# Landing margins in a planner's model, and an earlier place for the attention: a windowed-attention and MLP kernel on one Trainium2 core

## The chip, the cores and the metric

The kernel runs on one core of one Trainium2 chip. The core has five engines, each with its own instruction stream that is worked off in order: TensorE (PE) for matrix products and transposes, VectorE (DVE), ScalarE (ACT), GpSimd (POOL) and SyncE (SP). SP here only issues transfers (DMA); POOL issues transfers too. An instruction that waits for a semaphore holds everything behind it on the same engine. Inputs lie in HBM, work is done in the on-chip SBUF, and products arrive in eight PSUM banks of 2 KiB per partition.

The metric is the device time of one launch in microseconds (us). The median of three runs before the change is 238.64 us (238.53 to 239.28).

## The reference

The inputs are `q`, `k`, `v` of shape (4, 8, 768, 64): 4 batches, 8 heads, 768 positions, head size 64. Then come two weights, `moe_w_in` (512 x 2048) and `moe_w_out` (2048 x 512).

```
scores = q @ k^T / sqrt(64)
keep   = (key < 4) or (0 <= query - key < 128)      # 4 sink keys and a window of 128
a      = softmax(where(keep, scores, -1e9))
x      = (a @ v), heads side by side: 3072 tokens x 512
out    = relu(x @ w_in)^2 @ w_out                   # 3072 x 512, float32
```

## The kernel before, in words

**Work.** A batch is worked in three parts `s` = 0, 1, 2 of 256 positions. For a part and a half of the heads (`m0` = 0 or 2: two pairs of heads `m`), the kernel forms the scores of the window only (`scores`, L571, PE), takes the exponential of each pair (L590, ACT), multiplies it by the triangle mask (`domask`, L599 on DVE or L221 on POOL), forms the values together with a column of ones that gives the denominator (`values`, L632, PE), and divides (`norm`, L643 and L644, DVE). The four sink keys of all heads are gathered into a small block `kblk` (`sink_keys`, L509, two small DVE copies), scored against all later queries by one product (`sink_scores`, L530, PE), and their exponentials `es` (L539, ACT) join `values` for `s` > 0. The result `xn_sb` has to be transposed into `xT`. Then `layer1` (L691, PE; relu L700; square L707) makes the hidden values for parts 0 and 1 together (512 tokens, eight steps) and for part 2 (256 tokens, four steps), and `layer2` (L731) makes the output in 24 steps of four matmuls each per batch, which are copied out and stored (L747).

**Two ways to get q, k and v in.** Batches 0 and 1 load them as float32 through SP (L339, L355), cast them, and transpose on PE (L468); their `xn_sb` is transposed on PE too (`bridge`, L668). Batches 2 and 3 (`NATURAL`) take another way: POOL loads them with a cast in the transfer (`load_natural`, L372 for q and k into `qn`, L381 for v; 18 transfers a batch), SP transposes each of 12 tiles by a transfer (`turn`, L426, `qkT<-qn`), and SP transposes `xn_sb` by a transfer as well (`turn_x`, L655, `xT<-xn_sb`, two per part; in the planner the second one comes after the first has landed).

**What sets the order.** Nothing is scheduled by hand or by the compiler. The kernel describes its steps as `Op`s in a `Plan`, each with the engines that can do it and their costs in us, the steps it comes after, the PSUM and SBUF slots that it takes and gives back, and a key. `Plan.run` simulates time: again and again it picks, among the steps whose predecessors are done, the one that can start earliest, and among equal starts (to 0.01 us) the one with the lowest key. The step is then emitted, so the order of picking is the order of every engine's stream on the chip. A step's end in the model decides when its readers can be picked. For a transfer the model takes the issue, then `DMA_START` (1.2 us on SP, 1.6 on POOL), then its own duration on its queue (0.3 us for a transpose, 64 x 0.032 = 2.05 us for a natural load), and then `DMA_LATENCY` = 0.9 us. A transpose is thus seen as landed 1.25 + 1.2 + 0.3 + 0.9 = 3.65 us after its issue begins.

**Keys.** Batch `b` has `layer1` at `b` to `b` + 0.5 and `layer2` at `b` + 0.5 to `b` + 1, 1/48 of a batch per step. The attention of batch `b` + 1 is woven into this, with a place `f` of each step between 0 and 1.05 and the key `b` + LO + (HI - LO) x `f`, LO = 0.05 and HI = 0.9. For part `s` and half `m0`, `scores` have `f` = 0.36 + `s`/6 + 0.08 `m0`, `values` 0.16 more, and `turn_x` of the part stands at 0.36 + `s`/6 + 0.36. `sink_keys` stand at 0.1, `sink_scores` at 0.4. The attention of batch 1 has keys of its own, without LO and HI.

Of the kernel before, what the change touches and what calls it, by code (L numbers as in the profile page):

```python
# [19 lines left out]
DMA_LATENCY = 0.9  # L20
# [3 lines left out]
class Slot:  # L24
# [3 lines left out]
    def __init__(self, pools, readers):  # L28
        self.pools = (pools,) if isinstance(pools, str) else pools
        self.pool, self.readers, self.end = self.pools[0], readers, 0.0  # L30


class Op:
    def __init__(self, key, engines, run, after, takes, reads, dma, follow):
        self.key, self.engines, self.run = key, engines, run
        self.after, self.takes, self.reads, self.dma = list(after), list(takes), list(reads), dma
        self.follow, self.yields = list(follow), []
        self.end = self.issued = None


class Plan:

# [12 lines left out]
    def run(self):  # L57
        free = {p: [0.0] * n for p, n in self.capacity.items()}
        engine = {}
        queue = {}  # L60
        waiting = list(self.ops)
        blockers = {id(o): len(o.after) + len(o.follow) for o in waiting}
        landed = {}
        users = {}
        for o in waiting:
            for a in o.after + o.follow:
                users.setdefault(id(a), []).append(o)
        ready = [o for o in waiting if not blockers[id(o)]]
        for o in ready:
            o.at = 0.0  # L70
        left = len(waiting)
        while left:
            best = None
            for o in ready:
                t = o.at
                need = {}
                for s in o.takes:
                    if len(s.pools) > 1:
                        s.pool = min(s.pools, key=lambda p: min(free[p], default=1e9))
                    need[s.pool] = need.get(s.pool, 0) + 1  # L80
                ok = True
                for p, n in need.items():
                    if len(free[p]) < n:
                        ok = False
                        break
                    t = max(t, sorted(free[p])[n - 1] + LATENCY)
                if not ok:
                    continue
                if o.dma:
                    past = landed.get(next(iter(o.engines)), ())  # L90
                    if len(past) >= 8:
                        t = max(t, past[-8])
                pick = None
                for e, c in o.engines.items():
                    slack = PE_SLACK if e == "pe" and t > 0 else 0.0
                    start = max(t + slack, engine.get(e, 0.0))
                    if pick is None or start + c < pick[1] + pick[2]:
                        pick = (e, start, c)
                cand = (round(pick[1], 2), o.key)
                if best is None or cand < best[0]:  # L100
                    best = (cand, o, pick)
            assert best is not None, "no op can run"
            _, o, (e, start, cost) = best
            ready.remove(o)
            left -= 1
            for s in o.takes:
                free[s.pool].sort()
                free[s.pool].pop(0)
            self.now, self.gap = start, start - engine.get(e, 0.0)
            o.run(e)  # L110
            engine[e] = start + cost
            end = start + cost
            if o.dma:
                moved = [y.end - DMA_LATENCY for y in o.yields]
                queue[e] = max([queue.get(e, 0.0), end + DMA_START[e]] + moved) + o.dma
                end = queue[e] + DMA_LATENCY
                landed.setdefault(e, []).append(end)
            o.end, o.issued = end, start + cost
            for s in o.reads:
                s.readers -= 1  # L120
                s.end = max(s.end, end)
                if not s.readers:
                    free[s.pool].append(s.end)
            for u in users.get(id(o), ()):
                blockers[id(u)] -= 1
                if not blockers[id(u)]:
                    u.at = max([a.end + LATENCY for a in u.after] + [a.issued for a in u.follow])
                    ready.append(u)
        return max(o.end for o in self.ops)
# [3 lines left out]
def kernel(  # L133
# [145 lines left out]
    def dma_op(queue, name, run, us, behind=None, takes=(), yields=()):  # L279

        def go(e):
            ds = run(e)
            if behind is not None:
                for d in ds:
                    after_dma(d, loaded[behind])
            loaded[name] = ds[-1]
        o = op(-5, {queue: (0.85 if queue == "pool" else 0.5) + (0.3 if behind else 0.0)}, go, dma=us, takes=takes,
               follow=[chained[queue]] if queue in chained else (),
               after=[ops[behind]] if behind is not None else ())
        ops[name] = chained[queue] = o  # L290
        o.yields += [ops[y] for y in yields]
        o.follow += [ops[y] for y in yields]
        return o
# [17 lines left out]
    ops, late = {}, {}  # L311
# [48 lines left out]
    def load_natural(b, s, older_values):  # L360

        begun = [ops["layer1", b - 2, 0, 0], w_out_op[3]]
        for ti in (1, 0):
            if s == 0:
                qn_slot[b, ti] = Slot("qr", NT)
            for i in range(2):
                t = 2 * s + i

                def run(e, t=t, ti=ti):
                    if t == 0:  # L370
                        qn_t[b, ti] = work["qr"].tile([128, NT, DM], BF16, name="qn", tag="qr")
                    return [nc.gpsimd.dma_start(  # L372
                        out=qn_t[b, ti][:, t, :].rearrange("p (h d) -> p h d", d=D),
                        in_=(q, k)[ti][b, :, 128 * t:128 * t + 128, :].rearrange("h p d -> p h d"))]
                o = dma_op("pool", ("qk", b, ti, t), run, 64 * 0.032,
                           ("v", 1, 3) if (b, ti, t) == (2, 1, 0) else None,
                           [qn_slot[b, ti]] if t == 0 else ())
                o.after += begun
        for t in (2 * s, 2 * s + 1):
            def run(e, t=t):  # L380
                return [nc.gpsimd.dma_start(  # L381
                    out=v_sb[b % 2][:, t, :, 0:D],
                    in_=v[b, :, 128 * t:128 * t + 128, :].rearrange("h p d -> p h d"))]
            o = dma_op("pool", ("v", b, t), run, 64 * 0.032)
            o.after += begun + older_values

    def load_sinks(queue, b):
        eng = nc.scalar if queue == "act" else nc.sync
# [3 lines left out]
    def attention(b, key):  # L392
# [16 lines left out]
        def stage(g, f0, f1, side):  # L409
# [9 lines left out]
            if b in NATURAL:  # L419
                for s in range(NS):  # L420
                    for ti in (1, 0):
                        for i in range(2):
                            t = 2 * s + i

                            def turn(e, s=s, ti=ti, i=i, t=t):
                                nc.sync.dma_start_transpose(  # L426
                                    out=qkT_sb[:, :, ti, t, :], in_=qn_t[b, ti][:, t, :])
                            ops["turn", b, ti, t] = op(
                                at(0.1 * s), {"sp": 1.25}, turn, dma=0.3, reads=[qn_slot[b, ti]],
                                after=[ops["qk", b, ti, t]] + prev_scores + prev_sinks)  # L430
                            copies.append(ops["turn", b, ti, t])
                    ops["cast", b, s] = ops["v", b, 2 * s + 1]
            w = 2 if b == 0 else 1
# [112 lines left out]
            for s in range(t0 // 256, last // 256):  # L546
                fs = 0.36 + 0.5 * (256 * s - t0) / (last - t0)
                norms = []
                for m0 in (0, 2):
# [36 lines left out]
                    o = 0 if s else 128  # L586
# [65 lines left out]
                if b in NATURAL:  # L652
                    for t in (2 * s, 2 * s + 1):
                        def turn_x(e, t=t):
                            nc.sync.dma_start_transpose(out=xT[:, t // 2, :, 128 * (t % 2):128 * (t % 2) + 128],  # L655
                                                        in_=xn_sb[:, t, :])
                        o_ = op(at(fs + 0.36), {"sp": 1.25}, turn_x, dma=0.3, after=norms + older_layer1 +
                                ([o_] if t % 2 else []))
                    ops["bridge", b, s] = ops["xT", b, s] = o_
                    continue  # L660
                bx = Slot(side, 1)
# [132 lines left out]
    for b in range(1, B):  # L794
        load_sinks("sp", b)

    LO, HI = 0.05, 0.9
    for b in range(B):
        if b == 0:
            at = attention(0, lambda f: f - 1.0)  # L800
# [62 lines left out]
```

## Time and profile before

| what | value |
|---|---|
| median of three runs | 238.64 us (238.53 to 239.28) |
| the profiled execution: its time, its span | 240.36 us, 238.7 us |
| PE busy | 220.0 us, 92% of the span |
| ACT, DVE, POOL busy | 113.0, 103.8, 57.2 us |
| mean granted TensorE clock | 0.981 |
| longest waits of PE | 4.2 us (on `xn_sb`), 3.0 us (on `xT`) |

The span runs from the first to the last instruction of the profiled execution; its time is 1.66 us longer than the span, and 1.72 us longer than the median of the runs. The time axis of every row that is quoted is the profiled execution's, in us from the start of the span. By that axis batch 0 begins its MLP at about 19 us, batch 1 at 84, batch 2 at 139.5 and batch 3 at 188.

In rows that name a wait, the part behind `<-` is what ended it. `DMA a<-b` is a transfer that writes tile a from b, counted from its issue to its landing. `SPq` is SP's issuing of transfers.

### The profile page before, as it was taken

How to read it: one execution, taken by the hardware profiler on the slowest of the kernel's cores; microseconds unless marked ns; L12 is line 12 of the kernel's file. 1: busy time of each engine (PE TensorE's matmuls, PEld its weight loads, DVE VectorE, ACT ScalarE, POOL GpSimd, SP SyncE). 2: the span in 40 equal slices, each digit the busy share in tenths (PEclk: the TensorE clock that was granted, in tenths of full speed). 3: DMA queues.
4: the chain of work that ended last, by engine and by line, in shares of the span. 5: the costliest groups of instructions: out<-in, count | busy, mean ns of one | idle time of the engine just before them, and what ended most of it. 6: DMA issues, size and time to landing. Idle time of an engine off the chain costs nothing.

```text
span 238.7 us, 4545 instructions
## 1 busy us (share of the span) xinstructions
PE 220.0 (92%) x1918; PEld 140.0 (59%) x1940; DVE 103.8 (44%) x186; ACT 113.0 (47%) x126; POOL 57.2 (24%) x85
## 2 busy tenths in 40 slices
PE   7889999999983999999999869999999999999991
PEld 6458984568851655596455444578545545784440
DVE  6563435359755357455316414466403323340010
ACT  2495565427882085575334444759403346550110
POOL 5184016033986507982002000000000000000000
PEclk9999999999998899999999979999999999999998
DMA  5999969999999999999844732010005312000051
GB/s 170 270 180 208 214 169 202 276 368 215 228 146 118 152 158 193 165 151 132 56 88 127 149 122 44 3 29 18 0 0 136 109 23 91 0 0 3 0 220 45
DMA packets 84101, 29.70 MB, mean 124 GB/s; under 512 B 70256, under 2 KB 80496, under 8 KB 84080
## 3 DMA queue, kind: packets, MB, share of 16 engines
q0 software_dynamic: 40128, 8.92, 43.4%
q1 hardware_dynamic: 43912, 20.48, 38.2%
q8 instruction: 15, 0.25, 0.5%
q14 instruction: 6, 0.05, 0.1%
q10 hardware_dynamic: 40, 0.01, 0.0%
HBM read 27.30 MB, written 6.29 MB: 141 GB/s over the span
## 4 chain that ended last, share of the span: by engine, by line
PE 65%; DMA 19%; ACT 5%; SPq 4%; DVE 3%; issue 2%; ACTq 0%; DVEq 0%; POOLq 0%
PE pm L691 29%; PE py L731 25%; PE po L632 5%; DMA qr<-in_q_dram 5%; DMA qr<-in_k_dram 4%; DMA qkT<-qn 4%; PE ps L571 3%; DMA w_out_sb<-in_moe_w_out_dram 2%; DMA qn<-in_k_dram 2%; ACT r L700 2%; DMA vf<-in_v_dram 2%; ACT expm L590 2%; SPq L339 2%; SPq L426 1%; DMA xT<-xn_sb 1%
## 5 line engine op out<-in xcount | busy, mean ns | idle before, releaser
L691 PE MATMUL pm<-xT,w_in_sb 128*128 128x256 bf16 (+1 forms) x576 | 88.2, 311 | 3.2 <-DMA xT<-xn_sb 3.0
L731 PE MATMUL py<-w_out_sb,gT 128*128 128x512 bf16 x365 | 87.0, 382 | 1.8 <-issue 0.8
L691 PEld LDWEIGHTS <-w_in_sb 128*128 128x128 bf16 x576 | 63.0, 114 | 24.2 <-issue 5.4
L700 ACT ACTIVATE r<-pm 128x1024 bf16<-128x1024 f32 x48 | 49.2, 1026 | 43.6 <-PE pm L691 35.2
L731 PEld LDWEIGHTS <-gT 128*128 128x128 bf16 x384 | 35.8, 98 | 40.0 <-issue 2.7
L590 ACT ACTIVATE expm<-ps 128x1024 bf16<-128x1024 f32 (+1 forms) x48 | 43.3, 955 | 18.1 <-PE ps L571 18.1
L707 DVE TENSOR_TENSOR gT<-r 128x1024 bf16<-128x1024 bf16 x48 | 33.4, 696 | 42.3 <-ACT r L700 42.3
L599 DVE TENSOR_TENSOR expm<-expm,mask 128x1024 bf16<-128x1024 bf16 (+1 forms) x37 | 24.2, 662 | 22.4 <-ACT expm L590 21.8
L205 ACT ACTIVATE osb<-py 128x1024 f32<-128x1024 f32 (+1 forms) x10 | 9.6, 960 | 39.6 <-PE py L731 33.0
L632 PEld LDWEIGHTS <-expm 128*128 128x128 bf16 x352 | 18.0, 101 | 5.5 <-issue 1.6
L632 PE MATMUL po<-v,expm 128*128 128x65 bf16 x352 | 19.1, 198 | 0.3 <-DVE v L207 0.2
L644 DVE TENSOR_TENSOR xn_sb<-po,rc 128x512 bf16<-128x512 f32 x24 | 16.6, 692 | 0.8
L643 DVE RECIPROCAL rc<-po 128x8 f32<-128x8 f32 x24 | 4.9, 204 | 26.4 <-PE po L632 26.3
L571 PE MATMUL ps<-qkT 64*128 64x128 bf16 (+1 forms) x256 | 14.7, 238 | 0.1
L632 PE MATMUL po<-vs,es 128*128 128x65 bf16 x128 | 14.4, 200 | 0.0
L571 PEld LDWEIGHTS <-qkT 64*128 64x128 bf16 x256 | 8.0, 94 | 10.2 <-issue 9.2
L209 POOL CAST qs<-qr 128x512 bf16<-128x512 f32 (+1 forms) x9 | 6.7, 743 | 29.6 <-DMA qr<-in_k_dram 21.9
L207 DVE COPY osb<-py 128x1024 f32<-128x1024 f32 (+2 forms) x4 | 3.6, 891 | 23.1 <-PE py L731 23.1
L632 PEld LDWEIGHTS <-es 128*128 128x128 bf16 x128 | 12.4, 102 | 0.0
L372 POOL DMA_DIRECT2D qn<-in_k_dram x12 | 10.9, 924 | 2.8 <-DMA vf<-in_v_dram 1.4
L372 POOL DMA_DIRECT2D qn<-in_q_dram x12 | 10.9, 916 | 1.8 <-DMA qn<-in_k_dram 1.8
L381 POOL DMA_DIRECT2D v<-in_v_dram x12 | 10.6, 894 | 2.7 <-DMA qn<-in_q_dram 2.7
(49 smaller groups left out, 99.7 us busy)
## 6 DMA issues: line engine op xcount, KB each, us to landing
out_dram<-osb SPq DMA_DIRECT2D x11, 512.0 KB, 4.6
vf<-in_v_dram SPq DMA_DIRECT2D x12, 256.0 KB, 4.9
w_in_sb<-in_moe_w_in_dram POOLq DMA_DIRECT2D x4, 512.0 KB, 8.1
w_out_sb<-in_moe_w_out_dram POOLq DMA_DIRECT2D x4, 512.0 KB, 10.3
qr<-in_k_dram SPq DMA_DIRECT2D x6, 256.0 KB, 4.3
qr<-in_q_dram SPq DMA_DIRECT2D x6, 256.0 KB, 4.5
qr<-in_k_dram SPq DMA_DIRECT2D x2, 768.0 KB, 5.2
qr<-in_q_dram SPq DMA_DIRECT2D x2, 768.0 KB, 6.8
```

What stands on the lines that cost most here:

```text
L205: nc.scalar.activation(out=dst, in_=src, func=AF.Copy)
L372: return [nc.gpsimd.dma_start(out=qn_t[b, ti][:, t, :].rearrange("p (h d) -> p h d", d=D), in_=(q, k)[ti][b, :, 128 * t:128 * t + 128, :]. ...
L381: return [nc.gpsimd.dma_start(out=v_sb[b % 2][:, t, :, 0:D], in_=v[b, :, 128 * t:128 * t + 128, :].rearrange("h p d -> p h d"))]
L571: nc.tensor.matmul(ps[:, h2, o:o + w], lhsT=qkT_sb[r, m, 1, c, :], rhs=qkT_sb[r, m, 0, qb:qb + w // 128, :], start=(i == 0 and not biased) ...
L590: nc.scalar.activation(out=x[:, :, o:512], in_=bank_t["s", b, s, m][:, :, o:512], func=AF.Exp, scale=scale)
L599: nc.vector.tensor_mul(x[:, :, o:512], x[:, :, o:512], mk[:, :, o:512])
L632: nc.tensor.matmul(pv[:, i, h2, :], lhsT=lhsT, rhs=rhs, start=(n_ == 0), stop=(n_ == len(mms) - 1))
L644: nc.vector.tensor_tensor(out=xn_sb[:, 2 * s:2 * s + 2, 128 * m0:128 * m0 + 256].rearrange("p i (j h d) -> p j i h d", j=2, d=D), in0=pv[: ...
L691: nc.tensor.matmul(pm[:, i, :], lhsT=w_in_sb[:, fb // 4, kb, fb % 4:512:4], rhs=xT[:, c0 // 256:(c0 + cw) // 256, kb, :], start=(kb == 0), ...
L700: nc.scalar.activation(out=r, in_=bank_t.pop(tag), func=AF.Relu)
L707: (nc.vector if e == "dve" else nc.gpsimd).tensor_mul(gT_sb[c0 // 512][:, fbs[0]:fbs[0] + n, c0 % 512:c0 % 512 + cw], r, r)
L731: nc.tensor.matmul(pm[:, i, :], lhsT=gT_sb[t // 4][:, fb, 128 * (t % 4):128 * (t % 4) + 128], rhs=w_out_sb[:, fb, :], start=(fb == 0), sto ...
```

## The change

The planner's `Op` gets a field `margin`, in us, zero unless set, which `Plan.run` adds to the end of a transfer. It is set to 2.0 for every natural load (L372, L381), to 4.0 for every `turn` (L426) and to 1.5 for every `turn_x` (L655). HI goes from 0.9 to 0.75, so the keys of the attention of batches 2 and 3 go over 0.70 of a batch and no longer over 0.85. No instruction is added or removed by this; only the order of the streams, and the choice between two engines where a step has one, can differ.

```
-        self.follow, self.yields = list(follow), []
+        self.follow, self.yields, self.margin = list(follow), [], 0.0
...
                 queue[e] = max([queue.get(e, 0.0), end + DMA_START[e]] + moved) + o.dma
-                end = queue[e] + DMA_LATENCY
+                end = queue[e] + DMA_LATENCY + o.margin
                 landed.setdefault(e, []).append(end)
...
                 o.after += begun
+                o.margin = 2.0
...
             o.after += begun + older_values
+            o.margin = 2.0
...
                             ops["turn", b, ti, t] = op(
                                 at(0.1 * s), {"sp": 1.25}, turn, dma=0.3, reads=[qn_slot[b, ti]],
                                 after=[ops["qk", b, ti, t]] + prev_scores + prev_sinks)
+                            ops["turn", b, ti, t].margin = 4.0
...
                         o_ = op(at(fs + 0.36), {"sp": 1.25}, turn_x, dma=0.3, after=norms + older_layer1 +
                                 ([o_] if t % 2 else []))
+                        o_.margin = 1.5
...
-    LO, HI = 0.05, 0.9
+    LO, HI = 0.05, 0.75
```

More of the change, by code (lines that the diff above doesn't have):

```diff
@@ L36, in __init__ @@
         self.after, self.takes, self.reads, self.dma = list(after), list(takes), list(reads), dma
-        self.follow, self.yields = list(follow), []
+        self.follow, self.yields, self.margin = list(follow), [], 0.0
         self.end = self.issued = None
@@ L115, in run @@
                 queue[e] = max([queue.get(e, 0.0), end + DMA_START[e]] + moved) + o.dma
-                end = queue[e] + DMA_LATENCY
+                end = queue[e] + DMA_LATENCY + o.margin
                 landed.setdefault(e, []).append(end)
@@ L378, in load_natural @@
                 o.after += begun
+                o.margin = 2.0
         for t in (2 * s, 2 * s + 1):
@@ L385, in load_natural @@
             o.after += begun + older_values
+            o.margin = 2.0
     def load_sinks(queue, b):
@@ L430, in stage @@
                                 after=[ops["qk", b, ti, t]] + prev_scores + prev_sinks)
+                            ops["turn", b, ti, t].margin = 4.0
                             copies.append(ops["turn", b, ti, t])
@@ L658, in stage @@
                                 ([o_] if t % 2 else []))
+                        o_.margin = 1.5
                     ops["bridge", b, s] = ops["xT", b, s] = o_
@@ L795 @@
         load_sinks("sp", b)
-    LO, HI = 0.05, 0.9
+    LO, HI = 0.05, 0.75
     for b in range(B):
```

## The prediction, made before the changed kernel was run

> **What bounds the kernel now.** I read the page first, then who waited for whom on PE, then a table of the span by stretches, and last the chain that ended last around the two long waits.
>
> ```profile
> PE 220.0 (92%) x1918; PEld 140.0 (59%) x1940; DVE 103.8 (44%) x186; ACT 113.0 (47%) x126; POOL 57.2 (24%) x85
> ```
>
> ```profile
> PE px L668 <- DVE xn_sb L644: 4.2, 1, 4.2
> PE pm L691 <- DMA xT<-xn_sb: 3.0, 1, 3.0
> ```
>
> PE works 92% of the span; beside its own weight loads, which overlap, nothing reaches half of it, so PE's idle time and slow clock are what an order can win. Two waits stand out, one occurrence each. The table (busy time of PE, PEld, DVE, ACT and POOL, then the granted clock) shows what else is left:
>
> ```profile
> 71.30:75.40 4.10, 0.00 (x0) 0.00 (x0) 1.87 (x6) 0.75 (x1) 3.01 (x4) 1.00 2.44 149
> 75.40:79.20 3.80, 3.68 (x36) 2.53 (x38) 1.23 (x3) 1.02 (x1) 1.80 (x3) 0.56 1.42 103
> 79.20:136.50 57.30, 56.65 (x517) 33.91 (x523) 28.23 (x49) 29.13 (x32) 21.02 (x25) 1.00 1.49 137
> 136.50:139.50 3.00, 0.05 (x2) 0.09 (x1) 1.38 (x3) 2.13 (x3) 0.00 (x0) 1.00 0.47 102
> 139.50:147.20 7.70, 7.69 (x49) 4.32 (x49) 2.12 (x4) 2.05 (x2) 0.00 (x0) 0.78 0.31 92
> ...
> 184.00:196.00 12.00, 11.47 (x80) 5.98 (x79) 3.67 (x6) 5.62 (x6) 0.00 (x0) 1.00 0.28 73
> ```
>
> After each long wait the clock is low (0.56 for 3.8 us, 0.78 for 7.7 us). The quiet stretches idle 0.65 us in 57.3 and 0.53 us in 12.0, so the prize is these two places. PE's own rows there give the waits to two places:
>
> ```profile
> 75.43 0.65 PE L668 MATMUL px<-ident,xn_sb 128*128 128x128 bf16 x8 [4.17 <-DVE xn_sb L644]
> ...
> 139.51 2.40 PE L691 MATMUL pm<-xT,w_in_sb 128*128 128x512 bf16 x8 [2.96 <-DMA xT<-xn_sb]
> ```
>
> The chain at the first:
>
> ```profile
> 64.99 8.44 DMA qkT<-qn
> 73.46 0.16 DVE kblk L509
> ...
> 73.83 0.69 DVE expm L599
> ...
> 74.68 0.70 DVE xn_sb L644
> ...
> 76.08 1.71 PE py L731 x4
> 77.78 1.32 PE po L632 x24
> ...
> 80.13 0.73 PE po L632 x24
> 80.86 1.73 PE py L731 x8
> ```
>
> Batch 2's first transpose lands 8.44 us after its issue. `sink_keys` of batch 2 stands on DVE ahead of a mask and a norm of batch 1, and waits for that landing. The mask, the norm and then PE's transposes of batch 1 stand behind it, though none needs it. On DVE and ACT:
>
> ```profile
> 73.46 0.35 DVE L509 COPY kblk<-qkT 64x16 bf16<-64x16 bf16 x2 [4.60 <-DMA qkT<-qn]
> ```
>
> ```profile
> 67.33 1.95 ACT L590 ACTIVATE expm<-ps 128x1024 bf16<-128x1024 f32 x2
> 70.11 1.94 ACT L590 ACTIVATE expm<-ps 128x1024 bf16<-128x1024 f32 x2 [0.84 <-PE ps L571]
> ```
>
> DVE was idle from 73.46 - 4.60 = 68.86, and the mask's exponential, the first of the two from 67.33, was done at about 68.3. The second place:
>
> ```profile
> 127.31 0.55 PE ps L571 x12
> ...
> 129.69 0.73 PE po L632 x24
> ...
> 133.08 1.22 SPq L655
> ...
> 134.39 1.22 SPq L426
> ...
> 135.70 1.22 SPq L426
> ...
> 136.97 2.50 DMA xT<-xn_sb
> ...
> 141.92 1.32 PE po L632 x24
> 143.24 3.97 PE pm L691 x16
> ```
>
> `layer1` of batch 2 needs the four `turn_x` of parts 0 and 1. The last `values` of part 1 (129.69) are late; then SP issues one `turn_x` at 133.08, two turns of batch 3, and the last `turn_x` at 136.97, which lands 2.50 us later. PE had nothing else left by then: it is busy for 0.05 us of the stretch from 136.5 to 139.5.
>
> **The change, part by part.** *What is added or removed:* no instruction. All that follows is order.
>
> *Price of the first wait.* PE stood 4.17 us, from 71.26 to 75.43. The four matmuls behind it took 1.71 us where eight take 1.73, so 0.85 too much; the 24 of `values` took 1.32 where the later 24 took 0.73, 0.59 too much. Together 4.17 + 0.85 + 0.59 = 5.61 us.
>
> *Margins on loads and turns.* In the planner's model, `sink_keys` become ready 2.0 (the natural load of k) + 4.0 (the turn) = 6.0 us later. The old model gives a turn 3.65 us; the trace gave 8.44. So the model took the landing for 4.79 us earlier than it was, in the trace's time at 73.43 - 4.79 = 68.6, which is just where DVE began to idle. With 6.0 more it is 74.6, after the true landing. In the 4.60 us from 68.86 DVE then finds the mask (0.69), reciprocal and norm (from the mask's end at 74.52 to 75.38, 0.86) and two masks whose exponentials end at 70.11 + 1.94 = 72.05: two times 0.69 more. These 2.9 us fit before 74.6, so I expect all of them to pass `sink_keys`. What is late next: `sink_keys` run at about 73.5 to 74.6 with nothing of batch 1 behind them that PE already waits for, since the norm then behind them needs `values`, which need those masks. PE finds `xn_sb` ready at 68.86 + 0.69 + 0.86, about 70.4, before it asks at 71.26. From both sides: nothing is gained if `sink_keys` stay in front, 5.61 us if the wait goes. I take 5.61, because the shift (6.0) is larger than the model's error (4.79).
>
> The same 6.0 us move everything else that reads a turn of batches 2 and 3, `scores` and `sink_scores`. Could that starve a later step? The rows:
>
> ```profile
> 104.97 0.86 PE pk L530 x4
> ...
> 119.88 0.73 PE po L632 x24
> ...
> 147.21 0.86 PE pk L530 x4
> ...
> 167.19 0.72 PE po L632 x24
> ```
>
> The sink scores of batch 2 run 14.9 us before the first `values` that use them (119.88, part 1), those of batch 3 20.0 us before (167.19). Six us later still leaves 9 and 14, so I cost it at nothing; without that cover it would be up to 6 us a batch. Where PE comes 5.61 us earlier to the sink scores, being placed later protects it from the last turns of batch 2. On POOL the loads are modelled as landed 2.0 us later, so a mask there may pass one load issue; on SP, stores and `turn_x` may pass a turn. Both only shift work that has us to spare (in the row from 136.5 POOL does nothing any more).
>
> *HI from 0.9 to 0.75, and the margin on `turn_x`.* Price of the second wait: PE stood 2.96 us; then 8 matmuls of the same 512 columns took 2.40 for 1.73, 0.67 too much; 24 of `values` 1.32 for 0.73, 0.59; 16 matmuls 3.97 for twice 1.73, 0.51. With 2.96 that is 4.73 us.
>
> The last `values` of part 1 stand at f = 0.36 + 0.167 + 0.16 + 0.16 = 0.847. Their key falls by 0.15 x 0.847 = 0.127 of a batch, 6.1 steps of `layer2` (1/48 each) of 0.86 us (1.73 for eight matmuls), so 5.3 us earlier against `layer2`; their `scores` move 0.15 x 0.687 x 48 = 4.9 steps. Every instruction of the step moves: six score products a part on PE, exponentials on ACT, masks on DVE or POOL, norms, and the `turn_x` on SP, which come before some turns of batch 3. Against it goes the margin of 1.5: the second `turn_x` of a part is planned after the first has landed, so one more turn (1.22 us) can slip between. Net 5.3 - 1.2 = 4.1 us, against 2.96 needed. Can the engines deliver it? Between the first scores of batch 2 (100.92, next fence) and those of the half in question (123.20) lie three halves, 7.4 us each, while one needs about 0.55 + 1.94 + 0.69 + 0.73 + 0.86 = 4.8 on PE, ACT, DVE, PE and DVE in turn. The room, 3 x 2.6 = 7.8, is more than 5.3. From both sides: nothing, or 4.73. I take 4.73: the same change of batch from 2 to 3 (184 to 196) runs with 0.53 us idle, so a batch change without a wait exists, and I charge that 0.53 here.
>
> ```profile
> 100.92 0.44 PE ps L571 x8
> ...
> 123.20 0.55 PE ps L571 x12
> ```
>
> **Sum.** The profiled execution takes 240.36 us (span 238.7 and 1.66 around it) and the median is 238.64, 1.72 lower. 240.36 - 5.61 - 4.73 + 0.53 = 230.55 profiled; 230.55 - 1.72 = 228.8 for the median.
>
> **The rivals.** *The second wait stays, chance 0.16.* The margins push `scores` of batches 2 and 3 back by as much as HI pulls them forward (6.0 against 5.3 us) and the extra turn on SP does the rest: only the first wait goes, 238.64 - 5.61 = 233.0. For it: the terms are alike in size. Against it: the sink scores wait for all twelve turns of their batch and run at 104.97, so every turn had landed 18 us before the `scores` at 123.20; keys and not landings hold these. The Trainium skill speaks for this rival: "DMA: Bandwidth & Descriptors", section "Anatomy of one DMA — SWDGE (gpsimd) path", gives a transfer a fixed cost of about 2.0 us and its bytes at 436 GB/s, which is an estimate of 2.3 us for a turn's 128 KB, and by it a margin of 4 is time thrown away. The `turn_x` agree with the page, the turns do not, by this table of issues with the median to landing:
>
> ```profile
> qkT<-qn SPq DMA_TRANSPOSE x24, 7.3
> xT<-xn_sb SPq DMA_TRANSPOSE x12, 2.4
> ```
>
> A second rule prices what may remain. The low clock followed a wait of only 2.96 us in these rows, so a remainder of the wait may keep its 1.77 us of slow clock. The Trainium skill, "TensorE: Matmul & The Clock Gate", section "What's actually happening", has the clock fall only after an idle window of about 3.4 us; by it a rest of 2.96 us or less costs itself alone, and this rival would end at 233.0 - 1.77 = 231.2. I give that 0.03 of the 0.16, since the rows speak against it.
>
> *The first wait stays, chance 0.08.* `sink_keys` stay ahead of the mask, because the model of DVE is behind or ahead of the chip at that point: 238.64 - 4.73 + 0.53 = 234.4. For it: only 1.2 us lie between shift and error.
>
> *The change does not do what it says, 0.05.* Other steps fill the same holes and both waits stay: 238.6.
>
> *Slower, 0.09.* The attention is pulled into fewer us than its chain needs, and PE, in order, stands in front of `values` until exponentials and masks are done. From the end of scores at 123.75 the two exponentials and the second mask lead to 126.81, so `values` can't start for 3.06 us:
>
> ```profile
> 124.16 1.94 ACT L590 ACTIVATE expm<-ps 128x1024 bf16<-128x1024 f32 x2
> ```
>
> ```profile
> 126.12 0.69 DVE L599 TENSOR_TENSOR expm<-expm,mask 128x1024 bf16<-128x1024 bf16 x1 [0.23 <-ACT expm L590]
> ```
>
> With only two `layer2` steps (1.73) in between, 1.33 us are left for each of 12 halves in batches 2 and 3: 16.0 us, 244.8. It decides from (5.61 + 4.73 - 0.53) / 12 = 0.82 us a half. Against it: the planner picks by earliest start and puts 1.04 us for an exponential and 0.75 for a mask, above the rows (0.97, 0.69), so it fills this gap before it looks at keys.
>
> **How the numbers follow.** Forecast 0.62, and the four rivals as given. Faster by over 0.3% (0.7 us, about what a measurement of this kernel can tell): 0.62 + 0.16 + 0.08 = 0.86; within it 0.05; slower 0.09. The range begins at 227.0: the sum without the 0.53, and with the 0.65 us of idle in the long quiet stretch gone as well, is 227.6, and durations vary a little. It ends at 235.0 to hold both cases in which one wait stays; that leaves out 0.14.
>
> **What would show it.** In the profile after: the wait of PE for `xn_sb` at 71 gone and no DVE wait of `kblk` on `qkT` over about 1 us; the clock at 1.00 between 72 and 84; `layer1` of batch 1 beginning at about 79; no wait of `layer1` on `xT`, with `layer2` of batch 1 still running when the last `turn_x` of part 1 lands; batch 2's `layer1` beginning near 139.5 - 5.6 - 3.0 = 131. PE's busy time would fall by the slow-clock part, 0.85 + 0.59 + 1.77 = 3.2, to about 217. Wrong would be: a new wait of PE over 1 us on `ps`, `expm` or `qkT` between 85 and 190, or on a turn's landing at `sink_scores`.

## The result, and the profile after

The changed kernel takes 230.12 us (229.33 to 230.80) where the kernel before takes 238.96 us beside it: a ratio of 0.9616, 95% interval 0.9559 to 0.9674. The prediction's 228.8 over 238.64 is 0.9588, inside that interval.

The line of busy times, and who waited on PE, after (the columns as before; the changed file's lines are 3 to 5 higher, so L571 is now L575, L691 is L696, L731 is L736, L426 is L429 and L655 is L659):

```profile
PE 217.9 (95%) x1919; PEld 139.7 (61%) x1940; DVE 104.2 (46%) x186; ACT 113.2 (50%) x126; POOL 57.3 (25%) x85
```

```profile
PE pm L696 <- DMA xT<-xn_sb: 1.0, 1, 1.0
...
PE px L673 <- DVE xn_sb L648: 0.4, 1, 0.4
```

Where waits of 4.2 and 3.0 us stood, 0.4 and 1.0 us are left. The span went from 238.7 to 228.6. The table by stretches (busy time of PE, PEld, DVE, ACT and POOL, then the granted clock):

```profile
71.30:79.00 7.70, 7.08 (x92) 4.47 (x92) 3.19 (x8) 2.99 (x4) 4.67 (x6) 1.00 2.60 120
79.00:131.80 52.80, 52.43 (x484) 31.50 (x486) 27.94 (x47) 29.51 (x33) 21.38 (x26) 1.00 1.66 153
131.80:133.00 1.20, 0.15 (x4) 0.09 (x2) 0.90 (x2) 0.40 (x1) 0.00 (x0) 1.00 0.45 91
133.00:140.00 7.00, 7.00 (x39) 3.57 (x40) 2.50 (x4) 4.37 (x5) 0.00 (x0) 1.00 0.49 131
```

The clock stays at 1.00 behind both places, where it was 0.56 and 0.78. Not all of the profiled gain of 10.1 us belongs to the change. The end is one part: from the last product to the end of the span there were 238.7 - 233.43 = 5.3 us, and now there are 228.6 - 224.26 = 4.3, with nothing in that stretch that the change moves. First the kernel before, then after, in the chain:

```profile
223.76 9.67 PE py L731 x44
```

```profile
214.59 9.67 PE py L736 x44
```

The start of the span adds almost nothing: PE's last four matmuls of `layer2` ahead of the first place start at 70.22 us before and at 70.08 after. PE's rows, before and then after, with the first `layer1` product of batch 1 last:

```profile
70.22 1.04 PE L731 MATMUL py<-w_out_sb,gT 128*128 128x512 bf16 x4
...
84.38 3.62 PE L691 MATMUL pm<-xT,w_in_sb 128*128 128x512 bf16 x16
```

```profile
70.08 1.04 PE L736 MATMUL py<-w_out_sb,gT 128*128 128x512 bf16 x4
...
70.96 0.61 PE L673 MATMUL px<-ident,xn_sb 128*128 128x128 bf16 x8
...
78.86 3.62 PE L696 MATMUL pm<-xT,w_in_sb 128*128 128x512 bf16 x16
```

These rows cut the kernel at three points. Call *stretch 1* the time from the four matmuls to `layer1` of batch 1, and *stretch 2* the time from there to the end of the last product. Stretch 1 fell from 14.16 to 8.78 us, stretch 2 from 149.05 to 145.40. The medians fell by 8.5 (238.64 to 230.12) to 8.8 us.

**The first place.** The chain after:

```profile
65.37 9.39 DMA qkT<-qn
...
74.78 0.16 DVE kblk L513
...
76.24 0.70 DVE xn_sb L648
...
76.99 0.51 PE px L673 x6
...
79.02 3.45 PE pm L696 x16
```

```profile
69.46 0.69 DVE L648 TENSOR_TENSOR xn_sb<-po,rc 128x512 bf16<-128x512 f32 x1
71.03 0.73 DVE L603 TENSOR_TENSOR expm<-expm,mask 128x1024 bf16<-128x1024 bf16 x1 [0.88 <-ACT expm L594]
71.94 0.69 DVE L603 TENSOR_TENSOR expm<-expm,mask 128x1024 bf16<-128x1024 bf16 x1 [0.19 <-ACT expm L594]
74.78 0.35 DVE L513 COPY kblk<-qkT 64x16 bf16<-64x16 bf16 x2 [2.15 <-DMA qkT<-qn]
```

In DVE's rows the first norm (done at 70.15, its mask begun at 68.62) and two masks now run ahead of `sink_keys`. These still wait, 2.15 us, because the turn landed even later (9.39 us after issue), and the two norms behind them cost PE 0.41 us. This is not the old wait made shorter: the eight transposes for which PE waited 4.17 us now run at 70.96 without a wait, and the 0.41 us stand ahead of the transposes of the next part. `layer1` of batch 1 begins at 79.02 in the chain.

**The second place.** DVE's last norm of part 1, then the chain, then PE's own row:

```profile
123.46 0.69 DVE L648 TENSOR_TENSOR xn_sb<-po,rc 128x512 bf16<-128x512 f32 x1
```

```profile
125.64 2.08 SPq L429
...
127.82 1.21 SPq L429
...
129.12 1.22 SPq L429
...
130.39 2.48 DMA xT<-xn_sb
```

```profile
132.92 3.65 PE L696 MATMUL pm<-xT,w_in_sb 128*128 128x512 bf16 x16 [1.05 <-DMA xT<-xn_sb]
```

The norm is done at 123.46 + 0.69 = 124.15 and the first `turn_x` is issued at once (124.17). Then three turns of batch 3 stand between it and the second, where there were two, and PE waits 1.05 us.

These rows allow the second wait to be split. Call *lead* the time from the end of that norm to PE's arrival at `layer1` of batch 2, that is, the work PE still has, and *SP's time* the time from the norm to the landing of the second `turn_x`. The wait is SP's time less the lead. Before, the norm ended at 130.84 + 0.69 = 131.53, PE arrived at 139.51 - 2.96 = 136.55 and the landing was at 139.47: lead 5.0, SP's time 7.9, wait 2.9.

### The profile page after: what moved, and what is told of

Read it like the earlier page. It is cut to its first block, busy times and chain, and to the rows that moved or that the text cites. A ratio compares the mean times of both kernels' runs of the same rounds, so it can differ in the third digit from the quotient of the medians.

```text
span 228.6 us, 4552 instructions
## 1 busy us (share of the span) xinstructions
PE 217.9 (95%) x1919; PEld 139.7 (61%) x1940; DVE 104.2 (46%) x186; ACT 113.2 (50%) x126; POOL 57.3 (25%) x85
## 4 chain that ended last, share of the span: by engine, by line
PE 72%; DMA 16%; SPq 5%; POOL 2%; DVE 2%; issue 1%; ACT 1%; ACTq 0%; POOLq 0%
PE pm L696 30%; PE py L736 30%; DMA w_out_sb<-in_moe_w_out_dram 6%; PE po L636 4%; DMA qkT<-qn 4%; PE ps L575 4%; DMA qr<-in_q_dram 2%; DMA qr<-in_k_dram 2%; SPq L429 2%; SPq L340 2%; PE pk L534 1%; POOL w_in_sb L300 1%; SPq L356 1%; PE pt L472 1%; DMA xT<-xn_sb 1%
## 5 line engine op out<-in xcount | busy, mean ns | idle before, releaser
L696 PE MATMUL pm<-xT,w_in_sb 128*128 128x256 bf16 (+1 forms) x576 | 87.2, 308 | 1.3 <-DMA xT<-xn_sb 1.0
L736 PE MATMUL py<-w_out_sb,gT 128*128 128x512 bf16 x366 | 86.4, 379 | 1.5 <-issue 0.5
L696 PEld LDWEIGHTS <-w_in_sb 128*128 128x128 bf16 x576 | 62.7, 114 | 21.6 <-issue 1.5
L736 PEld LDWEIGHTS <-gT 128*128 128x128 bf16 x384 | 35.6, 98 | 39.8 <-issue 2.1
L603 DVE TENSOR_TENSOR expm<-expm,mask 128x1024 bf16<-128x1024 bf16 (+1 forms) x37 | 24.8, 677 | 19.9 <-ACT expm L594 19.3
L636 PEld LDWEIGHTS <-expm 128*128 128x128 bf16 x352 | 16.7, 97 | 4.5 <-issue 0.5
L636 PE MATMUL po<-v,expm 128*128 128x65 bf16 x352 | 17.7, 193 | 0.2 <-DVE v L208 0.2
L575 PE MATMUL ps<-qkT 64*128 64x128 bf16 (+1 forms) x256 | 14.7, 238 | 0.1
L575 PEld LDWEIGHTS <-qkT 64*128 64x128 bf16 x256 | 8.0, 94 | 10.4 <-issue 9.4
L636 PE MATMUL po<-vs,es 128*128 128x65 bf16 x128 | 13.1, 193 | 0.0
L636 PEld LDWEIGHTS <-es 128*128 128x128 bf16 x128 | 11.7, 97 | 0.0
```

Of the source, the lines that this page charges most:

```text
L575: nc.tensor.matmul(ps[:, h2, o:o + w], lhsT=qkT_sb[r, m, 1, c, :], rhs=qkT_sb[r, m, 0, qb:qb + w // 128, :], start=(i == 0 and not biased) ...
L603: nc.vector.tensor_mul(x[:, :, o:512], x[:, :, o:512], mk[:, :, o:512])
L636: nc.tensor.matmul(pv[:, i, h2, :], lhsT=lhsT, rhs=rhs, start=(n_ == 0), stop=(n_ == len(mms) - 1))
L696: nc.tensor.matmul(pm[:, i, :], lhsT=w_in_sb[:, fb // 4, kb, fb % 4:512:4], rhs=xT[:, c0 // 256:(c0 + cw) // 256, kb, :], start=(kb == 0), ...
L736: nc.tensor.matmul(pm[:, i, :], lhsT=gT_sb[t // 4][:, fb, 128 * (t % 4):128 * (t % 4) + 128], rhs=w_out_sb[:, fb, :], start=(fb == 0), sto ...
```

## The experiments

The lead, SP's time and the two stretches of every kernel, in us, from the same rows of its trace (where PE does not wait, its arrival is the start of its first `layer1` product of batch 2, and the landing is taken 2.5 us after the issue):

| kernel | first wait | lead | SP's time | second wait | stretch 1 | stretch 2 | median us | ratio to before, 95% interval |
|---|---|---|---|---|---|---|---|---|
| before | 4.17 | 5.0 | 7.9 | 2.96 | 14.16 | 149.05 | 238.6 to 241.0 | |
| sinkkeys_only | 0 | 5.0 | 7.8 | 2.79 | 8.19 | 147.36 | 233.80 | 0.9753 (0.9679 to 0.9826) |
| sinkscores_late | 0.5 | 6.9 | 8.6 | 1.83 | 8.87 | 146.18 | 230.64 | 0.9592 (0.9529 to 0.9656) |
| turn4_only | 0.9 | 6.9 | 8.4 | 1.62 | 9.47 | 145.98 | 231.76 | 0.9641 (0.9566 to 0.9716) |
| land_only | 0 | 6.9 | 8.3 | 1.53 | 8.19 | 145.86 | 230.62 | 0.9627 (0.9573 to 0.9681) |
| margins_only | 0 | 8.4 | 9.8 | 1.48 | 8.19 | 146.78 | 231.25 | 0.9701 (0.9637 to 0.9765) |
| hi_only | 4.35 | 7.7 | 8.0 | 0.38 | 15.33 | 144.32 | 235.38 | 0.9822 (0.9771 to 0.9873) |
| after | 0.4 | 7.7 | 8.7 | 1.05 | 8.78 | 145.40 | 230.12 | 0.9616 (0.9559 to 0.9674) |
| no_xmargin | 0 | 7.6 | 7.2 | 0 | 8.19 | 144.17 | 228.95 | 0.9561 (0.9501 to 0.9622) |
| xpair | 0.3 | 6.0 | 3.9 | 0 | 8.62 | 143.76 | 228.23 | 0.9575 (0.9512 to 0.9639) |
| turn6_xpair | 0 | 10.3 | 4.4 | 0 | 8.19 | 143.77 | 228.30 | 0.9572 (0.9510 to 0.9635) |
| hi60 | 0 | 11.1 | 6.1 | 0 | 8.19 | 143.79 | 228.29 | 0.9575 (0.9497 to 0.9653) |

The kernel before spreads from 236.59 to 241.69 us over these comparisons, the others from 0.3 to 1.5 us (sinkkeys_only 3.0), so the ratios are wide. The medians of two rows were not always taken on the same chip: sinkkeys_only, hi_only, land_only and no_xmargin ran on one, margins_only, xpair, turn6_xpair and hi60 on a second, sinkscores_late and turn4_only on a third. Two rows are therefore better compared by their stretches, which leave out the start and the last store. Each is of one execution. In sinkscores_late and turn4_only the first wait is one of `values` at the same place, for a mask.

**sinkkeys_only: one pair of copies moved.** The kernel before, with one more predecessor for `sink_keys` in the planner.

```
     A["sink_keys"] = op(at(0.1), {"dve": 0.25}, sink_keys,
-        after=([ops["turn", b, 1, 0]] if b in NATURAL else copies) + prev_sinks)
+        after=([ops["turn", b, 1, 0], ops["turn", b, 0, 1]] if b in NATURAL else copies) + prev_sinks)
```

> The kernel before, with no margins and HI 0.9; only the planner is told that sink_keys of batches 2 and 3 come after the fourth turn as well, so on DVE the two small copies stand four places later. PE, ACT, POOL and SP have the order of before. Theory (head of line on DVE): the wait of PE for xn_sb falls from 4.2 us to under 0.5 and its slow clock goes, the wait for xT stays near 3.0 with its slow clock; 238.8 - 5.6 = 233.2 us. Rival (the first wait went because of the wider shift, the mask on POOL ahead of a load or PE's order): the wait of 4 us stays, 238.8 us.

233.80 us, the first wait gone, the second as it was:

```profile
PE pm L696 <- DMA xT<-xn_sb: 2.8, 1, 2.8
```

PE's, ACT's, POOL's and SP's streams are those of before; only the places of `sink_keys` of batches 2 and 3 on DVE differ. So the first wait was head of line on DVE and nothing else: two copies of 0.17 us standing four steps later (a mask, a norm and two masks). Stretch 1 fell by 14.16 - 8.19 = 5.97 us, 2.5% of the span. The median fell by 2.5% too, of the whole change's 3.8%, but not by the first place alone: in the profiled execution the slow clock behind the second wait stayed away as well (stretch 2 is 1.69 us shorter, see the last section), where it was expected to stay.

**hi_only: the earlier place without margins.**

```
-o.margin = 2.0 ; ops["turn", b, ti, t].margin = 4.0 ; o_.margin = 1.5
+all 0.0, HI = 0.75
```

> All margins 0, HI 0.75. Theory (the two waits are separate; keys act on the second): the wait for xn_sb stays near 4.2 us with its slow clock, the wait for xT falls from 3.0 to 1 or less; 238.8 - 4.2 = 234.6 us, between 234 and 236. Rival (the landing margins freed the second wait, keys are worth nothing): both waits stay, 238.8 us.

235.38 us, the reverse picture:

```profile
PE px L673 <- DVE xn_sb L648: 4.3, 1, 4.3
...
PE pm L696 <- DMA xT<-xn_sb: 0.4, 1, 0.4
```

HI alone raises the lead from 5.0 to 7.7 us and leaves the first wait alone. PE's rows show what the lead is made of. Between the norm and the arrival stood four steps of `layer2` before and six now (one matmul's record is missing in each), and the 24 `values` of part 2 now run ahead of `layer1` too.

**land_only: margins on loads and turns alone.**

```
-o_.margin = 1.5 ; HI = 0.75
+o_.margin = 0.0 ; HI = 0.9
```

> Margins 2.0 on natural loads and 4.0 on turns, none on turn_x, HI 0.9. Theory: the wait for xn_sb goes (under 0.5), the wait for xT stays at 2 to 3 us with its slow clock; 233 to 234 us. Rival (the landing margins free both waits): 229 to 230.5 us with the wait for xT at 1 or less.

230.62 us, far under the range expected. Here the rival won half: the first wait went, but the second fell to 1.5 us too, with HI still at 0.9. The lead is 6.9, against 5.0: one step of `layer2` and the 24 `values` of part 2 more. The order of the score products on PE shows where these 1.8 us come from. Before, the two halves of part 0 of batch 2 (x8 each) stand on either side of the sink scores (100.92, then L530 at 104.97, both shown above, then):

```profile
109.33 0.44 PE ps L571 x8
```

With the landing margins, in the chain:

```profile
94.80 0.44 PE ps L575 x8
...
98.86 0.44 PE ps L575 x8
...
102.91 0.86 PE pk L534 x4
```

The gap between the halves fell from 8.4 to 4.1 us. In the kernel's text the attention of batch 2 has two PSUM slots, of two banks each. The sink scores take one of them until their exponential is done, and a half's scores need both; standing first, they kept the second half out. That the order is the cause, the next run shows; that the slots make the order is read from the kernel, and no run gave a third slot.

**sinkscores_late: that order alone.** As sinkkeys_only, with one line more.

```
     ops["scores", b, s, ms[0]] = sc[-1]
+    if (b, s, m0) == (2, 0, 2):
+        ss.after.append(sc[-1])
```

> As the run with only the sink_keys moved (no margins, HI 0.9), and in addition the planner puts the sink scores of batch 2 behind the second half's scores of part 0. Theory (the landing margins lengthen PE's lead only because the sink scores, which hold one of the two PSUM banks of the attention, no longer stand between the two halves of part 0): the lead grows from 5.0 to about 6.9 us, the wait for xT falls from 2.8 to 1 to 1.5, 230.6 us, as with the landing margins. Rival (the lead came from the margins on the turns as a whole, or from the loads): lead 5.0, wait 2.8, 233.8 us.

230.64 us, lead 6.9, and the order in the chain is that of land_only:

```profile
95.27 0.44 PE ps L575 x8
...
99.32 0.44 PE ps L575 x8
...
103.38 0.86 PE pk L534 x4
```

The wait is 1.8 us and not 1 to 1.5, as SP's time came out at 8.6. Two steps of the planner put elsewhere, with no margin and HI at 0.9, give what the landing margins give, to 0.7 us in stretch 1 and 0.3 in stretch 2.

**turn4_only: 4.0 on turns, nothing on the loads.**

```
-o.margin = 2.0 ; o_.margin = 1.5 ; HI = 0.75
+o.margin = 0.0 ; o_.margin = 0.0 ; HI = 0.9
```

> Only the margin of 4.0 on turns, HI 0.9, no other margin. It is smaller than the model's error of 4.8 us, so sink_keys pass the mask and the norm but stand ahead of the two masks of the next half. Theory: DVE waits there for the landing for 2.5 to 3.5 us, PE loses 0.3 to 1 us at the values of that half, the rest is as with both landing margins; 230.8 to 231.6 us. Rival (the 2.0 us on the loads are not needed): PE loses nothing there, 230.6 us or less. Second rival (4.0 is too little): the wait of 4 us comes back, 234 us or more.

231.76 us, 0.2 over the range expected. DVE, then PE:

```profile
73.76 0.43 DVE L513 COPY kblk<-qkT 64x16 bf16<-64x16 bf16 x2 [3.52 <-DMA qkT<-qn]
74.22 1.29 DVE L603 TENSOR_TENSOR expm<-expm,mask 128x1024 bf16<-128x1024 bf16 x2
```

```profile
74.97 0.23 PE L636 MATMUL po<-v,expm 128*128 128x65 bf16 x2 [0.86 <-DVE expm L603]
```

`sink_keys` pass the first mask and norm but stand ahead of the next two masks, and PE pays 0.86 us. The 2.0 us on the loads are what carries `sink_keys` past these.

**margins_only: all margins, HI at 0.9.**

```
-HI = 0.75
+HI = 0.9
```

> All three margins, HI 0.9. By the runs so far the wait for xT is SP's time from the last norm of part 1 to the landing of its second turn_x, less PE's lead (work left on PE after that norm). Theory: lead as with the landing margins alone (6.9 us), SP's time longer by a third turn (8.3 + 1.2 = 9.5), so the wait is 2 to 3 us, with or without a slow clock; 231.5 to 234 us. Rival (with the margins in place neither HI nor the margin on turn_x matters): the wait stays at 1.0 to 1.5, 230.5 us.

231.25 us. PE's waits in this stretch:

```profile
PE pm L696 <- DMA xT<-xn_sb: 1.5, 1, 1.5
PE ps L575 <- ACT expm L594: 0.9, 1, 0.9
```

The wait for `xT` was expected at 2 to 3 us and is 1.5, as the rival had it; the time lies between the two, 0.25 us below the range expected. SP's time came out as expected (9.8), the lead did not: it reads 8.4 and not 6.9, because eight more score products, and a wait of 0.9 us on them, stand before `layer1` and push PE's arrival back. Both waits together are 2.4 us. Against this kernel, HI at 0.75 brings 231.25 - 230.12 = 1.1 us by the medians and 1.4 in stretch 2.

**no_xmargin: the changed kernel without the margin on `turn_x`.**

```
-o_.margin = 1.5
+o_.margin = 0.0
```

> The changed kernel with the margin on turn_x at 0. Only SP's order differs: two turns of batch 3 and not three stand between the two turn_x of part 1 of batch 2. Theory (the rest of the second wait, 1.0 us, is the third turn on SP, 1.2 us): the last turn_x lands 1.2 us earlier, the wait for xT goes to about 0, 229.1 us. Rival (PE or the chain through ACT and DVE sets that point): the wait stays at 1.0, 230.1 us; if the margin protects something else, over 231.

228.95 us, and no wait for `xT`. Only SP's stream differs from that of the changed kernel; its rows:

```profile
123.45 1.34 SPq L659 DMA_TRANSPOSE xT<-xn_sb  x1
124.88 3.19 SPq L429 DMA_TRANSPOSE qkT<-qn  x2
128.12 1.26 SPq L659 DMA_TRANSPOSE xT<-xn_sb  x1
```

Two turns stand between, not three, SP's time is 7.2 instead of 8.7, and the lead of 7.6 covers it. The margin of 1.5 us made the kernel 1.2 us slower, by the medians and in stretch 2 alike (145.40 against 144.17). The 0.41 us of the first place are missing here too, though nothing differs there: the first turn landed sooner, and DVE waited 1.45 us for it and not 2.15.

**xpair, turn6_xpair and hi60: past the changed kernel.** In xpair the second `turn_x` follows the issue of the first, not its landing. turn6_xpair has, besides, 6.0 on the turns. hi60 is the changed kernel with HI at 0.6.

```
-after=norms + older_layer1 + ([o_] if t % 2 else []))
+after=norms + older_layer1, follow=[o_] if t % 2 else ())
```

> The changed kernel, but the planner may issue the second turn_x of a part right behind the first (it follows its issue, not its landing), so no turn of batch 3 stands between them. Theory (SP's order makes the rest of the second wait): SP's time from norm to landing falls from 8.7 to 4.5 to 6 us, the wait for xT is 0, 229.0 us, and no more than that, since PE has nothing else to win there. Rival (the turns of batch 3 come too late for its scores and sink scores, and PE waits there): 230 us or more, with a wait of PE on qkT or ps after 133.

> Margin of turns at 6.0 in place of 4.0, and the second turn_x right behind the first; HI 0.75. Theory: sink_keys of batch 2 pass the two norms as well, the wait of DVE for qkT (2.1 us in the changed kernel) and the 0.4 us of PE behind it go, and the wait for xT is 0; 228.4 to 228.8 us. Rival (two more us on every reader of a turn make batch 2 late): the lead shrinks and 230 us or more come out.

> The changed kernel with HI at 0.6 in place of 0.75. Theory (keys buy lead on PE, about half of what their arithmetic says): the lead grows from 7.7 to 9 to 10 us, over SP's 8.7, the wait for xT goes to 0, 229.0 us. Rival (the attention is pulled ahead of what ACT and DVE deliver, and PE stands in front of values): waits of PE on expm or po of over 1 us in sum, 231 us or more.

228.23, 228.30 and 228.29 us. They lie 0.1 to 0.8 us under what was expected. Each takes away the second wait, in its own way: xpair by SP's time (3.9 us, where 4.5 to 6 was expected), hi60 by the lead (11.1, where 9 to 10 was), with SP's time at 6.1 as well, turn6_xpair by both. In xpair SP's rows read:

```profile
123.87 3.27 SPq L659 DMA_TRANSPOSE xT<-xn_sb  x2
127.23 5.15 SPq L429 DMA_TRANSPOSE qkT<-qn  x4
```

That the three end within 0.1 us of each other, and within 0.03 us in stretch 2, is a floor: with no wait of PE above 0.3 us between 70 and 190, more lead or an earlier transpose has nothing to win. In turn6_xpair DVE's wait for `qkT` at the first place is gone as well. In xpair it is 1.7 us, and PE waits 0.26 us behind it: stretch 1 is 0.43 us longer there, which the medians do not show. The rival of too early an attention didn't show at HI 0.6.

## Why the prediction was right, and where its sizes were off

*The first wait* went as worked out: `sink_keys` were carried past the mask, the norm and two masks, and PE's transposes found `xn_sb` ready. Stretch 1 fell by 5.38 us, against 5.61 in the sum. One detail was wrong: `sink_keys` still wait, 2.15 us and not up to 1, since the landing came 9.39 us after the issue, and the step said that nothing behind them would matter; 0.41 us did. That part is chance: no_xmargin has the same streams up to there and loses nothing. Taken alone, in sinkkeys_only, this place brought 5.97 us.

*The slow clock* behind the two waits went. The sum had it as a fixed 1.44 and 1.77 us; it is not fixed. In sinkkeys_only it stayed away behind the second wait, and in hi_only the first place cost 15.33 - 8.19 = 7.1 us with a wait of 4.35 us, where before it cost 6.0 with one of 4.17.

*The second wait* was the term mis-sized. The step "so 5.3 us earlier against `layer2`" took the key's arithmetic for time: 6.1 steps of `layer2` by the keys were two steps in PE's rows (hi_only against before). HI at 0.75 raised the lead by 2.7 us without the margins (5.0 to 7.7) and by 0.8 with the landing margins in place (6.9 to 7.7). That fits the planner's rule, by which keys decide only among steps that could start at the same moment, but no run tried what else holds the steps back. Only at 0.6 did the lead grow to 11.1. The extra turn on SP was foreseen ("one more turn (1.22 us) can slip between") and cost 1.5 us of SP's time (7.2 in no_xmargin, 8.7 with it). So the wait went from 2.96 to 1.05 and not to the 0.53 us of a batch change without a wait, `layer1` of batch 2 began at 132.92 and not near 131, and stretch 2 fell by 3.65 us, against 4.73 - 0.53 = 4.20 in the sum.

*"I cost it at nothing"*, on moving the sink scores by 6 us, was wrong in the good direction: it raised the lead by 1.8 us through the order of sink scores and scores, of which the step had not thought. With that, the landing margins alone reach 230.62 us, and the gain of the second place belongs to them as much as to HI: HI and the margin on `turn_x` together add only 0.5 us to it in stretch 2 (145.86 to 145.40). The rival in which the margins push the scores back (233.0) had the sign of this term wrong.

*The rule of the Trainium skill* ("DMA: Bandwidth & Descriptors", "Anatomy of one DMA — SWDGE (gpsimd) path"), about 2.0 us and the bytes for a transfer, made the margin on turns look thrown away. The section fits transfers that GpSimd issues; all transposes here are issued by SP. Before, the twelve `turn_x` landed in 2.4 to 2.5 us, as by the estimate, and so did the one for which PE waits in the changed kernel (2.48); there, indeed, the margin of 1.5 costs 1.2 us. Others there took up to 5.4 us (median 3.3). For the turns the trace of the changed kernel has 9.39 us for the first; why they land late was not tried.

*The median* came out 1.3 us above the forecast, and more than the places is in this. They gave 5.61 - 5.38 + 4.20 - 3.65 = 0.8 us less than the sum. Yet the profiled execution took 230.28 us, below the 230.55 of the sum: by luck, since its end and its start were 1.0 us shorter for nothing that the change does. The step that failed for the median is "230.55 - 1.72 = 228.8". It carried over the 1.72 us by which the profiled execution before lay above its median, and in the changed kernel this distance is 230.28 - 230.12 = 0.16 us.

## What to carry to other kernels

When an order is made from a model, look for the wait whose model is wrong and ask what stands behind it on the same engine: here one landing modelled 4.8 us too early cost 2.5% of the time through two copies of 0.17 us that nothing of the batch then on PE needed. Split a late hand-over into the work that the bound engine still has and the time of the chain that must beat it; either term can be bought, and once one exceeds the other nothing more is to be had. Here a margin paid on transfers that land late, and cost time on one that lands sooner than modelled, where it let something else in between.

## What the runs showed of the hardware

The price of a wait of nearly 3 us varied by itself. Four runs of sinkkeys_only, whose remaining wait was 2.79 us in the profiled one:

```
span us   mean granted clock
230.5     1.000
231.2     0.993
233.0     0.987
233.5     0.981
```

In the profiled run of 231.2 us the clock behind the wait was 1.00; the low clock in its mean lies in the last 3.2 us of the span, behind all products. For the two longer runs no row shows where the clock was low, so that it was behind this wait is not shown.

```profile
130.80:133.60 2.80, 0.07 (x4) 0.11 (x1) 1.40 (x3) 2.15 (x3) 0.00 (x0) 1.00 0.48 100
133.60:138.00 4.40, 4.34 (x41) 2.65 (x41) 1.50 (x3) 1.02 (x1) 0.00 (x0) 1.00 0.30 115
```

In the profile of before it was 0.78 after 2.96 us. Slices of half a microsecond show both slow spells of that profile, from their first slice to their last (the granted clock is third from the end):

```profile
75.50:76.00 0.50, 0.50 (x9) 0.50 (x10) 0.50 (x2) 0.00 (x0) 0.50 (x1) 0.89 0.93 19
...
79.00:79.50 0.50, 0.29 (x3) 0.15 (x2) 0.32 (x2) 0.00 (x0) 0.11 (x1) 0.70 2.24 148
```

```profile
140.50:141.00 0.50, 0.50 (x4) 0.25 (x2) 0.00 (x0) 0.00 (x0) 0.00 (x0) 0.74 0.50 189
...
144.00:144.50 0.50, 0.50 (x4) 0.20 (x3) 0.50 (x2) 0.00 (x0) 0.00 (x0) 0.84 0.00 0
```

In all slices between these the clock is 0.50. A slice at 0.89 thus holds 0.11 us of half clock, and so on: the spells run from 75.89 to 79.30 and from 140.74 to 144.16, 3.4 us each. In hi_only the spell of the first wait is about twice as long, 73.7 to 80.5.

The Trainium skill ("TensorE: Matmul & The Clock Gate", "What's actually happening") names an idle window of about 3.4 us that runs freely. The length agrees, and the starts of the two spells lie 64.85 us apart, 19 such lengths. But no window was idle throughout: of the one that ended at 140.74, the wait of 2.96 us filled 2.2 us. Here the measurement decides: a wait shorter than a window may or may not be followed by a slow spell. Counted back in such lengths from the low clock at the end of sinkkeys_only (228.0), its wait of 2.79 us (130.87 to 133.66) was split over two windows, 1.6 and 1.2 us, and no slow spell followed. So chance may lie in where the wait falls on the windows; three waits are too few to show it, or to give a threshold.

The three kernels past the changed one, which have no such wait, spread by 0.7 us or less (xpair 228.11 to 228.78), the kernel before, with two, by 5.

SP needs 1.19 to 1.27 us to issue most transposes, but 47 of the 432 in the twelve traces took 1.8 to 3.0 us. Ten of the 47 stand right behind a store, as here before the change:

```profile
130.11 0.37 SPq L747 DMA_DIRECT2D out_dram<-osb  x1
130.59 2.40 SPq L426 DMA_TRANSPOSE qkT<-qn  x1
133.08 1.22 SPq L655 DMA_TRANSPOSE xT<-xn_sb  x1
```

Behind it, the first `turn_x` was issued 1.5 us after its norm was done (131.53). What makes an issue long was not tried.
